# One step of a two-layer recurrent transformer: where turned probabilities and weighted values stand in PSUM, where one addition stands on VectorE, and the order of a few loads and stores

## The chip, the cores and the metric

The kernel runs on one NeuronCore of a Trainium2 chip. TensorE (PE) multiplies matrices, VectorE (DVE) and ScalarE (ACT) copy, add and take exponentials, GpSimd (POOL) does small helper work, and SyncE (SP) issues nearly all DMAs, in the order in which they are written. Results of TensorE land in PSUM, which here is eight banks of 2 KB per partition. The metric is the time of one execution on the device in microseconds (us), and of several executions the median.

## The reference, cut to what matters

The input is a sequence of 2048 rows of width 512. Two layers A (with the same weights) and two layers B (with the same weights) follow each other, each behind a layer norm and with a residual:

```python
x = x + A(layernorm(x)); x = x + B(layernorm(x))
x = x + A(layernorm(x)); x = x + B(layernorm(x))
```

A walks over 64 segments of 32 rows and carries 8 rows of memory from one to the next, so its segments can't run at the same time:

```python
for s in range(64):
    h = concat([mem, xs])                  # 8 + 32 = 40 rows
    q, k, v = h @ Wq, h @ Wk, h @ Wv       # 32 heads of 128
    p = softmax(mask(q @ k.T * scale))     # 40 x 40 for each head
    o = (p @ v) @ Wo                       # 40 rows of 512
    mem, out = o[:8], o[8:]
```

B is a dense layer: `max(x @ w1, 0) @ w2`, with w1 of 512 x 1376.

## The kernel before

**Steps.** The two layers A are interleaved. Step k (`step`, from L920; step 0 is `first_step`, L872) works on segment k of the first A (called layer 0 in the code, a = 0) and on segment k - 3 of the second (a = 1). Between them the dense layer of row block k - 1 is computed in the same step. Steps 3 to 63 have both layers; steps 0 to 2 and 64 to 66 have one and are called `single`.

**A step on PE, in order.** `qk(0)` makes queries and keys of heads 0 to 15 (L570); `scores` (L604) and a softmax follow on DVE, ACT and POOL while PE does `qk(1)`, heads 16 to 31. The first half's probabilities are turned by a DMA (`turn_p`, L677, into `PT0`). PE goes on with `dense_h` (the first dense product, L513), the second half's scores, a late share of the output product (`output_late`, tile `wox`, L390), value products, and `dense_y` (the second dense product, L529). Then `turn_second` turns the second half's probabilities on PE by multiplying them with an identity (tile `tp`, L658) and copies them to `PT_sb` (L664). `weighted_v` multiplies probabilities and values (tiles `pv`, L696): 32 heads for each layer in three groups `PVS` of 12, 12 and 8 heads, heads 0 to 15 from `PT0`, 16 to 31 from `PT_sb`. `outputs` copies them out (L713): for each group the memory rows into `OTm`, then the token rows into `OTx`; with two layers DVE copies layer 0 and ACT layer 1. `output_mem` (tile `wo`, L612) needs all heads of `OTm` in order, and from its result `new_memory` makes the memory rows of the next step; until they are there, PE works on `output_own` (L390). Memory values (`memory_values`, L771) end the step and go through DRAM to reach the value buffer `Vs` in the layout that is wanted (L776, then L781).

**What sets the order.** PE, DVE, SP and POOL run in the order in which the code is written (`tc.manual_schedule`, L1071). ACT's order is planned by the framework. The framework adds a wait wherever an instruction touches a tile that another engine still writes or reads.

**PSUM.** Three banks rotate under the tag "c" (`ps_c`), two under "fill" (`ps_fill`), one holds `wox`, `wo` and some value products (`ps_wo`), and two hold the scores (`sp_banks`); the second of these also takes the dense result, and the first the weighted values of group 0, layer 1. A tile of a rotating pool waits until the tile that had its bank is read out. In a two-layer step `turn_second` uses four tiles of four slots, two of each pool; `weighted_v` puts group 0 (layer 0) and group 1 in "c" and group 2 in "fill". The four copies of turned tiles are ACT, ACT, ACT, DVE.

**Late additions.** `add_late` (L417) adds `wox` to the residual on DVE in two parts of 64 partitions (L423). In steps 4 to 65 both parts stand ahead of `turn_second`.

**The first steps on SP.** Before the dense weights are needed, their buffers `w1_sb` and `w2_sb` hold values on their way to DRAM: `values0` copies a product to such a slot and stores it (L344). Step 0 ends with five of these stores. Step 1 then issues the loads of its values (`load_values`, L741), two stores of memory values (L776), two dense weight loads (`load_w1(0, 1)`, L159), and the two loads of the memory rows (`load_memory_values`, L781), on which its `weighted_v` waits. Four loads of w2 (L162) end step 1. In step 2, which has one layer, `dense_h(1)` comes after a value group (L337).

Of the kernel before, what the change touches and what calls it, by code (L numbers as in the profile page):

```python
# [8 lines left out]
F32 = mybir.dt.float32  # L9
# [13 lines left out]
def kernel(  # L23
# [14 lines left out]
    nc = tc.nc  # L38
# [6 lines left out]
    L = M + SEG  # L45
# [4 lines left out]
    NC4 = Dm // 128  # L50
# [275 lines left out]

    def values0(p, n, lo=0, hi=NC4, pool=None, stage=None, late=False):
        r = 64 * (p % 2)
        if (n, lo) == (0, 0):
            vd0[p] = dram.tile([4, 2, 64, 512], BF, tag="vd0", bufs=6, name="vd0")  # L330
        if lo == 0:
            pool, tag = (pool, "wo") if pool else (ps_fill, "fill")
            vp_tiles[p, n] = pool.tile([128, 512], F32, tag=tag, name="vp")
        vp = vp_tiles[p, n]
        for c4 in range(lo, hi):
            for j in range(2):
                nc.tensor.matmul(vp[64 * j:64 * j + 64, :], lhsT=xT0[p // 2][:, c4, r:r + 64],  # L337
                                 rhs=Wv_sb[:, c4, (n + j) * 512:(n + j + 1) * 512],
                                 start=(c4 == 0), stop=(c4 == NC4 - 1), tile_position=(0, 64 * j))
        if hi < NC4:  # L340
            return
        vst = wk.tile([128, 512], BF, tag="vst", bufs=5, name="vst")[:] if stage is None else stage
        evict(vst, vp[:], late)
        nc.sync.dma_start(out=vd0[p][n // 2].rearrange("j t e -> (j t) e"), in_=vst)  # L344

# [298 lines left out]

    def turn_second(single=False):

        tps = {}
        for u in range(2):
            for g in range(2):
                if single and u:  # L650
                    tps[u, g] = tps[0, g][:, 4:8]
                    continue
                pool, tag = (ps_fill, "fill") if u else (ps_c, "c")
                tps[u, g] = pool.tile([128, 8 if single else 4, L], F32, tag=tag, name="tp")
            for sl in range(4):
                for g in range(2):
                    R = 64 * g
                    nc.tensor.matmul(tps[u, g][:, sl, :], lhsT=P1_sb[R:R + L, 4 * u + sl, :],  # L658
                                     rhs=ident[R:R + L, R:R + L], start=True, stop=True)
        ns = 8 if single else 4  # L660
        for s0 in range(0, 8, ns):
            for g in range(2):
                copy = nc.vector.tensor_copy if g and s0 == 8 - ns else nc.scalar.copy
                copy(out=PT_sb[:, s0:s0 + ns, g, :], in_=tps[s0 // 4, g][:, 0:ns])  # L664

# [206 lines left out]
    def first_step():  # L872
# [5 lines left out]
        with tc.high_priority(offset=PRIO):  # L878
# [19 lines left out]
            memory_values(0, (None, next(slots)), (1,))  # L898
            turn_second(True)
            tokens_in(1)  # L900
# [19 lines left out]
    def step(k):  # L920
# [9 lines left out]
        with tc.high_priority(offset=PRIO):  # L930
# [66 lines left out]
        with tc.high_priority(offset=PRIO):  # L997
# [71 lines left out]

    mom = {}  # L1070
    with tc.manual_schedule(engines={mybir.EngineType.PE, mybir.EngineType.DVE, mybir.EngineType.SP,  # L1071
# [82 lines left out]
```

## Time and profile before

| | |
|---|---|
| median of 3 runs | 1596.98 us (1592.14 to 1597.73) |
| profiled execution | 1600.23 us, of which the span of its instructions is 1598.5 |
| busy, share of the span | PE 98%, DVE 78%, ACT 47%, POOL 19% |
| mean granted TensorE clock | 0.999 of full speed |
| DMA | 144.17 MB, mean 90 GB/s |
| from one step's first turn (`tp`) to the next step's | 23.42 us where nothing disturbs it (937.72 to 961.13) |

A row of a timeline gives the start in us, the length in us, engine, line, operation, tiles as out<-in, shape, how many instructions were merged, and in brackets the idle time before it and what ended that. The rows of PE are modelled: a matmul's row reaches from the start of its input to the end of its output, some 0.18 us for 40 columns, while the next one may start 13 ns later. So the rate is read from starts. A row of stretches gives the stretch, its length, the busy time of PE, PEld, DVE, ACT and POOL with instruction counts, the granted clock, the DMA share and GB/s.

### The profile page before, as it was taken

The numbers are of one execution on the slowest core, as the hardware profiler recorded it, in microseconds if no ns is written. First come the engines' busy times: TensorE is split into PE (matmuls) and PEld (weight loads), VectorE is DVE, ScalarE is ACT, GpSimd is POOL, SyncE is SP. The second block draws the span as 40 slices with busy tenths as digits, with TensorE's granted clock in tenths as the row PEclk, the third lists the DMA queues.
The fourth block names the chain that finished last, engine by engine and source line by source line (L and its number), as shares of the span: only waits on it lengthen the run. The fifth ranks groups of instructions, "written<-read, shape, count | busy, mean of one in ns | idle before, by whom it ended". The sixth has DMA issues, their size and how long they took to land.

```text
span 1598.5 us, 104157 instructions
## 1 busy us (share of the span) xinstructions
PE 1562.6 (98%) x47089; PEld 1302.2 (81%) x47090; DVE 1245.6 (78%) x3526; ACT 745.8 (47%) x1878; POOL 299.8 (19%) x606
## 2 busy tenths in 40 slices
PE   6999999999999999999999999999999999999998
PEld 4678888878888888888887888888888888888876
DVE  4467888878887888887888888788878878878865
ACT  3444454444444445444544544444444454444442
POOL 2011122121112112212111211221211121121110
PEclk9999999999999999999999999999999999999999
DMA  9734234334333433433433434343233324324321
GB/s 370 225 80 82 77 77 89 87 70 87 80 80 82 84 85 71 90 82 73 92 79 78 81 88 81 72 94 80 75 85 76 81 74 85 80 71 86 73 68 39
DMA packets 233547, 144.17 MB, mean 90 GB/s; under 512 B 125032, under 2 KB 229520, under 8 KB 233104
## 3 DMA queue, kind: packets, MB, share of 16 engines
q1 hardware_dynamic: 233008, 137.48, 36.3%
q8 instruction: 369, 6.05, 1.7%
q14 instruction: 74, 0.61, 0.1%
q10 hardware_dynamic: 96, 0.03, 0.0%
HBM read 65.41 MB, written 45.09 MB: 69 GB/s over the span
## 4 chain that ended last, share of the span: by engine, by line
PE 87%; DVE 1%; DMA 1%; issue 1%; POOL 0%; ACT 0%; POOLq 0%; ACTq 0%
PE qp L570 35%; PE wo L612 7%; PE vm L771 7%; PE own L390 7%; PE v L376 6%; PE hp L513 5%; PE sp L529 4%; PE pv L696 4%; PE wox L390 4%; PE sp L604 3%; PE vp L811 3%; PE tp L658 1%; DMA xnT<-XN 1%; PE sp L696 0%; PE mt L835 0%
## 5 line engine op out<-in xcount | busy, mean ns | idle before, releaser
L576 ACT CAST QT<-qp 128x480 bf16<-128x480 f32 (+3 forms) x402 | 200.6, 499 | 394.1 <-PE qp L570 392.3
L570 PE MATMUL qp<-HT,Wq_sb 128*128 128x80 bf16 (+1 forms) x8576 | 368.2, 200 | 2.2 <-POOL HT L757 1.2
L570 PEld LDWEIGHTS <-Wq_sb 128*128 128x128 bf16 x8576 | 323.5, 100 | 33.8 <-issue 28.1
L570 PE MATMUL qp<-HT,Wk_sb 128*128 128x80 bf16 (+1 forms) x8576 | 344.3, 200 | 0.3 <-issue 0.3
L570 PEld LDWEIGHTS <-Wk_sb 128*128 128x128 bf16 x8576 | 317.1, 100 | 0.9 <-issue 0.8
L642 POOL TENSOR_TENSOR P_sb<-es,sm 128x320 bf16<-128x320 f32 x186 | 132.0, 724 | 698.2 <-ACT es L628 399.0
L578 DVE CAST KT<-qp 128x480 bf16<-128x480 f32 (+3 forms) x402 | 220.2, 574 | 28.4 <-PE qp L570 25.0
L622 DVE TENSOR_REDUCE mx<-sp 128x8 f32<-128x320 f32 x256 | 114.4, 487 | 131.1 <-PE sp L604 131.1
L390 PEld LDWEIGHTS <-OTx 128*32 128x32 bf16 x6272 | 157.7, 96 | 27.8 <-issue 10.9
L628 ACT ACTIVATE es<-es 128x320 f32<-128x320 f32 x256 | 109.4, 469 | 69.2 <-DVE es L626 69.1
L390 PE MATMUL own<-Wo_sb,OTx 128*32 128x256 bf16 x4096 | 133.0, 273 | 0.8 <-issue 0.6
L612 PE MATMUL wo<-Wo_sb,OTm 128*32 128x512 bf16 x2112 | 129.2, 383 | 1.4 <-issue 1.2
L771 PE MATMUL vm<-Wv_sb,HTm 128*32 128x512 bf16 x2144 | 129.1, 379 | 0.4 <-issue 0.3
L775 ACT CAST VmS<-vm 128x512 bf16<-128x512 f32 x132 | 77.4, 586 | 104.7 <-PE vm L771 100.8
L638 DVE TENSOR_REDUCE sm<-es 128x8 f32<-128x320 f32 x256 | 117.4, 458 | 10.8 <-ACT es L628 1.8
L376 PE MATMUL v<-Wv_sb,xnT 128*32 128x512 bf16 x2048 | 122.1, 379 | 0.1
L596 DVE CAST sp<-maskb 128x320 f32<-128x320 bf16 x256 | 118.5, 485 | 0.0
L626 DVE TENSOR_TENSOR es<-sp,mx 128x320 f32<-128x320 f32 x256 | 113.2, 482 | 0.5
L288 POOL TENSOR_TENSOR mv<-mv,mhalf_t 128x2 f32<-128x2 f32 (+1 forms) x67 | 45.7, 682 | 306.7 <-DVE mv L287 154.5
L513 PE MATMUL hp<-xnT,w_sb 128*128 128x64 bf16 (+1 forms) x2948 | 96.5, 192 | 0.8 <-DVE xnT L467 0.4
L529 PE MATMUL sp<-w_sb,hT 128*32 128x256 bf16 (+1 forms) x2772 | 92.9, 275 | 1.0 <-ACT hT L519 0.7
L771 PEld LDWEIGHTS <-HTm 128*32 128x32 bf16 x2144 | 59.8, 97 | 41.3 <-issue 2.3
(127 smaller groups left out, 2102.5 us busy)
## 6 DMA issues: line engine op xcount, KB each, us to landing
Vs<-vd SPq DMA_DIRECT2D x96, 256.0 KB
vd<-vst SPq DMA_DIRECT2D x133, 128.0 KB
vmd<-VmS SPq DMA_DIRECT2D x132, 128.0 KB
Vs<-vmd SPq DMA_DIRECT2D x254, 32.0 KB
Vs<-vmd SPq DMA_DIRECT2D x60, 128.0 KB
vd<-vst SPq DMA_DIRECT2D x96, 64.0 KB
Wq_sb<-in_A_Wq_dram SPq DMA_DIRECT2D x2, 2048.0 KB
Wk_sb<-in_A_Wk_dram SPq DMA_DIRECT2D x2, 2048.0 KB
```

The source lines that it names most:

```text
L376: nc.tensor.matmul(vp[32 * j:32 * j + 32, :], lhsT=tokens[c4], rhs=Wv_sb[:, c4, n * 512:(n + 1) * 512], start=(c4 == 0), stop=(c4 == NC4 - ...
L390: nc.tensor.matmul(t[q:q + 32, 0:HALF], lhsT=OTx[:, h, SEG * a:SEG * a + SEG], rhs=Wo_sb[:, h, HALF * j:HALF * j + HALF], start=(h < h0 + ...
L513: nc.tensor.matmul(hp[:, fc - f0, 0:n].rearrange("p (s t) -> p s t", s=ns), lhsT=w1_sb[:, c4, u:u + 128], rhs=cols(c4), start=(c4 == 0), s ...
L529: nc.tensor.matmul(sp_banks[1][32 * q:32 * q + 32, 0:w], lhsT=hT_tiles[d][0:fs, fc, SEG * o:SEG * o + SEG], rhs=w2_flat[0:fs, fc * Dm + HA ...
L570: nc.tensor.matmul(qp[:, hi, 0:ncol], lhsT=W_sb[:, c4, h * Dh:(h + 1) * Dh], rhs=HT[:, c4, a_lo:a_hi, :], start=(c4 == 0), stop=(c4 == NC4 ...
L576: nc.scalar.copy(out=dst[:, 0:nh, a_lo * L:a_hi * L], in_=qp[:, 0:nh, 0:ncol])
L578: nc.vector.tensor_copy(out=dst[:, 0:nh, a_lo * L:a_hi * L], in_=qp[:, 0:nh, 0:ncol])
L596: nc.vector.tensor_copy(out=sp_tiles[a], in_=maskb2)
L612: nc.tensor.matmul(wo[32 * j:32 * j + 32, :], lhsT=OTm[:, h, n, 2 * M * c:2 * M * c + 4 * M], rhs=Wo_sb[:, h, :], start=(h < 4), stop=(h > ...
L638: nc.vector.tensor_reduce(out=sm[:], in_=es[:], axis=AX.X, op=ALU.add)
L642: eng.tensor_tensor(out=P[:, :, 64 * a:64 * a + L], in0=es[:], in1=sm[:].unsqueeze(2).to_broadcast([128, 8, L]), op=ALU.mult)
L771: nc.tensor.matmul(vp[32 * j:32 * j + 32, :], lhsT=HTm[:, c4, :], rhs=Wv_sb[:, c4, n * 512:(n + 1) * 512], start=(c4 == 0), stop=(c4 == NC ...
```

## The change

- `turn_second`: two tiles of eight slots in "c" in every step. In two-layer steps the copies are, in order: ACT (tile 0, slots 0 to 3), DVE (tile 1, slots 0 to 3), ACT (tile 0, slots 4 to 7), ACT (tile 1, slots 4 to 7). What is given as `behind` is called after them.
- `weighted_v`: group 1 (heads 12 to 23) goes to "fill", group 2 to "c".
- `add_late`: the first part stays ahead of `turn_second`; the second stands behind its copies, in steps 4 to 65.
- `values0`: the five last stores of step 0 are kept back and issued in step 1, behind the memory-value stores; `load_memory_values` comes ahead of `load_w1(0, 1)`.
- The last two of four w2 loads move from the end of step 1 to step 2, behind `qk(0)`.
- In step 2 `dense_h` comes ahead of the second half of the value group.

The number and kinds of instructions stay the same on every engine.

```diff
-    def values0(p, n, lo=0, hi=NC4, pool=None, stage=None, late=False):
+    def values0(p, n, lo=0, hi=NC4, pool=None, stage=None, late=False, held=None):
...
-        nc.sync.dma_start(out=vd0[p][n // 2].rearrange("j t e -> (j t) e"), in_=vst)
+        def keep():
+            nc.sync.dma_start(out=vd0[p][n // 2].rearrange("j t e -> (j t) e"), in_=vst)
+        if held is None:
+            keep()
+        else:
+            held.append(keep)
...
-    def turn_second(single=False):
-        tps = {}
-        for u in range(2):
+    def turn_second(behind=None):
+        tps = [ps_c.tile([128, 8, L], F32, tag="c", name="tp") for g in range(2)]
+        for sl in range(8):
             for g in range(2):
-                if single and u:
-                    tps[u, g] = tps[0, g][:, 4:8]
-                    continue
-                pool, tag = (ps_fill, "fill") if u else (ps_c, "c")
-                tps[u, g] = pool.tile([128, 8 if single else 4, L], F32, tag=tag, name="tp")
...
-        ns = 8 if single else 4
-        for s0 in range(0, 8, ns):
-            for g in range(2):
-                copy = nc.vector.tensor_copy if g and s0 == 8 - ns else nc.scalar.copy
-                copy(out=PT_sb[:, s0:s0 + ns, g, :], in_=tps[s0 // 4, g][:, 0:ns])
+        if behind is None:
+            parts = ((0, 0, 8, nc.scalar.copy), (1, 0, 8, nc.vector.tensor_copy))
+        else:
+            parts = ((0, 0, 4, nc.scalar.copy), (1, 0, 4, nc.vector.tensor_copy),
+                     (0, 4, 8, nc.scalar.copy), (1, 4, 8, nc.scalar.copy))
+        for g, lo, hi, copy in parts:
+            copy(out=PT_sb[:, lo:hi, g, :], in_=tps[g][:, lo:hi])
+        if behind:
+            behind()
...
-                    pool, tag = (ps_fill, "fill") if t == 2 else (ps_c, "c")
+                    pool, tag = (ps_fill, "fill") if t == 1 else (ps_c, "c")
...
-                    values0(p, n, stage=next(slots))
+                    values0(p, n, stage=next(slots), held=held)
...
             qks = qk(0, act, behind=behind)
+            if k == 2:
+                load_w2(6, 8)
+                load_w2(8, 10)
...
             if k == 1:
+                for keep in held:
+                    keep()
+                load_memory_values(k, act)
                 load_w1(0, 1)
-                load_memory_values(k, act)
...
+        if k == 2:
+            dense_h(d)
         value_group(k, 0, 2, NC4, late=True)
...
-            if k > 1:
-                dense_h(d)
...
             dense_y(d, 0, NFC)
-            add_late(k)
-        else:
-            add_late(k, (0,))
+        add_late(k, (0,))
...
-            turn_second(single)
+            turn_second(None if single else lambda: add_late(k, (1,)))
+        if single and 1 < k < LAST:
+            add_late(k, (1,))
         if k == 1:
-            for lo, hi in ((0, 3), (3, 6), (6, 8), (8, 10)):
-                load_w2(lo, hi)
+            load_w2(0, 3)
+            load_w2(3, 6)
```

More of the change, by code (lines that the diff above doesn't have):

```diff
@@ L643, in softmax @@
                               in1=sm[:].unsqueeze(2).to_broadcast([128, 8, L]), op=ALU.mult)
-    def turn_second(single=False):
-        tps = {}
-        for u in range(2):
+    def turn_second(behind=None):
+        tps = [ps_c.tile([128, 8, L], F32, tag="c", name="tp") for g in range(2)]
+        for sl in range(8):
             for g in range(2):
-                if single and u:
-                    tps[u, g] = tps[0, g][:, 4:8]
-                    continue
-                pool, tag = (ps_fill, "fill") if u else (ps_c, "c")
-                tps[u, g] = pool.tile([128, 8 if single else 4, L], F32, tag=tag, name="tp")
-            for sl in range(4):
-                for g in range(2):
-                    R = 64 * g
-                    nc.tensor.matmul(tps[u, g][:, sl, :], lhsT=P1_sb[R:R + L, 4 * u + sl, :],
-                                     rhs=ident[R:R + L, R:R + L], start=True, stop=True)
-        ns = 8 if single else 4
-        for s0 in range(0, 8, ns):
-            for g in range(2):
-                copy = nc.vector.tensor_copy if g and s0 == 8 - ns else nc.scalar.copy
-                copy(out=PT_sb[:, s0:s0 + ns, g, :], in_=tps[s0 // 4, g][:, 0:ns])
+                R = 64 * g
+                nc.tensor.matmul(tps[g][:, sl, :], lhsT=P1_sb[R:R + L, sl, :],
+                                 rhs=ident[R:R + L, R:R + L], start=True, stop=True)
+        if behind is None:
[7 more added lines that the diff above has]
+            behind()
     def transpose_p():
@@ L898, in first_step @@
             memory_values(0, (None, next(slots)), (1,))
-            turn_second(True)
+            turn_second()
             tokens_in(1)
@@ L1068, in step @@
             prepare(k + 1)
-    mom = {}
+    mom, held = {}, []
     with tc.manual_schedule(engines={mybir.EngineType.PE, mybir.EngineType.DVE, mybir.EngineType.SP,
```

## The prediction

> **What bounds the kernel now.** I read the page first (busy shares, then the chain that ended last), then the timeline of one ordinary two-layer step engine by engine, then the first 90 us with the load queue and the granted clock.
>
> ```profile
> PE 1562.6 (98%) x47089; PEld 1302.2 (81%) x47090; DVE 1245.6 (78%) x3526; ACT 745.8 (47%) x1878; POOL 299.8 (19%) x606
> ...
> PE 87%; DVE 1%; DMA 1%; issue 1%; POOL 0%; ACT 0%; POOLq 0%; ACTq 0%
> ```
>
> PE is never idle for long and the chain runs over it, so whatever holds PE up is paid in full, once per step. PE rows are modelled, though: a matmul that waits can still look busy. So I read starts, not busy shares. One step, around its turned probabilities (tp, 961.13; below "+" counts us from there), first PE, then ACT, then DVE:
>
> ```profile
> 961.13 0.37 PE L658 MATMUL tp<-ident,P_sb 40*128 40x40 bf16 x16
> ...
> 961.78 0.45 PE L696 MATMUL pv<-PT,Vs 40*128 40x40 bf16 x8
> 962.07 0.56 PE L696 MATMUL pv<-PT_sb,Vs 40*128 40x40 bf16 x32
> 962.56 0.61 PE L612 MATMUL wo<-Wo_sb,OTm 128*32 128x512 bf16 x8
> ```
> ```profile
> 961.43 0.68 ACT L664 CAST PT_sb<-tp 128x160 bf16<-128x160 f32 x3 [0.82 <-PE tp L658]
> 961.99 0.27 ACT L713 CAST OTm<-sp 128x96 bf16<-128x96 f32 x1
> ```
> ```profile
> 960.47 0.88 DVE L423 TENSOR_TENSOR R<-R,wox 64x256 f32<-64x256 f32 x2
> 961.59 0.33 DVE L664 CAST PT_sb<-tp 128x160 bf16<-128x160 f32 x1 [0.24 <-PE tp L658]
> 961.87 0.26 DVE L713 CAST OTm<-pv 128x96 bf16<-128x96 f32 x1
> ```
>
> The 24 matmuls of heads 0 to 11 start between +0.22 and +0.53, one every 13 ns. Heads 12 to 15 (the x8) take from +0.65 to +0.92, where 0.10 would do: their two banks are those of the first turned tiles, and ACT frees them at +0.60 and +0.79. The x32 then run without a hole, every 12.4 ns, and wo starts at +1.43. The two additions (0.88) end before DVE is needed; DVE even waits 0.24. The first DVE copy of the weighted values, on which the first wo weights wait, ends at +1.00 (961.87 + 0.26): DVE has 0.43 us to spare before wo. This is the figure that decides.
>
> The start:
>
> ```profile
> 61.67 0.93 SPq L159 DMA_DIRECT2D w_sb<-in_B_w_dram  x2
> 63.04 0.69 SPq L781 DMA_DIRECT2D Vs<-vmd  x2
> ```
> ```profile
> 67.68 0.57 PE L696 MATMUL pv<-PT,Vs 40*128 40x40 bf16 x16 [1.74 <-DMA Vs<-vmd]
> ...
> 89.70 1.41 PE L529 MATMUL sp<-w_sb,hT 128*32 128x320 bf16 x22 [0.73 <-ACT hT L519]
> ```
> ```profile
> 69.40:72.80 3.40, 3.40 (x55) 1.98 (x48) 0.31 (x1) 0.59 (x1) 0.00 (x0) 0.50 0.89 292
> ```
>
> In step 1 PE waits 1.74 us for the memory rows of the values, which queue behind two dense-weight loads; soon after, the granted clock (third value from the end) is 0.50 for 3.4 us.
>
> **The change, part by part. Two-layer steps.**
>
> *Two banks instead of four.* Every turn now writes one of two whole-bank tiles, and in the built program the first ACT copy waits for the last turn of its tile, not for the fourth. Row for that: in step 1 the turned tile is already whole; turns start at 65.57, the ACT copy at 65.97, so +0.40 instead of +0.30. ACT's three copies (0.68 for three) would end at +1.08. But the third now reads the bank that DVE's copy reads, and the program makes it wait for that copy. The row comes first here: DVE's copy cannot start before +0.46 and takes 0.33, so it ends at +0.79; ACT's third starts about +0.82, takes 0.31 and ends at +1.13. [...]
>
> *Heads 12 to 23 in the fill banks.* Heads 12 to 15 wait for nothing (the value copies that hold these banks end before the turns start), so the 0.32 us hole closes. What is late next: head 16 needs ACT's first copy (+0.69) and head 17 DVE's (+0.79, +0.84 at PE: 0.05 is the lag seen where the second ACT copy, over at +0.79, lets its bank's matmul go at +0.84). Heads 17 to 24 run to about +1.0, head 25 waits for ACT's third copy: +1.13 + 0.05 = +1.18. Fourteen matmuls at 12.4 ns, then the usual 0.105 to wo: +1.45. So without the additions wo would come 0.02 us later than now: the hole only moves.
>
> *The second addition behind the copy.* It leaves a place where it cost nothing (dense matmuls hid it) and now stands between DVE's turned copy and DVE's first copy of weighted values. One addition is 0.42 (0.88 for two with the gap), and a gap of 0.03 stands on either side, as between the two in the 0.88, where today's two copies overlap by 0.05. Chain: 0.79 + 0.03 + 0.42 + 0.03 + 0.26 = +1.53, PE lag 0.05, wo at +1.57 to +1.58 instead of +1.43: **+0.147 us**. Queued behind the addition are all six DVE copies of weighted values; the later ones wait for PE anyway (DVE idles 0.34 before the second), so only the first counts, and all PE work after wo moves with it.
>
> I worked this out on all 62 steps that make the two additions, each with its own starts. 57 come out between +0.12 and +0.17. In three, where the additions already end late, the sum is +0.01 to +0.03. The two single-layer steps near the end gain 0.04 each, since DVE's copy no longer stands behind both additions. Sum **+8.4 us**. Ends: +0.02 per step if the addition finds cover (+1.1 in all); +0.18 if ACT's third copy lags more (+10.8). I take the chain, since each link is a row.
>
> *Step 1, load order.* Five held stores (128 KB each, issue 2.35 together) move on SP past one value load and two memory-value stores; the two memory-row loads move ahead of the two dense loads (344 KB each). Memory rows needed 4.6 us from issue (63.04) to use; 0.69 MB at the 337 GB/s of 70 to 72 us is 2.0 of that, leaving 2.6. Their issue cannot come before the two stores (end 60 to 61.6) plus 2.35, so 63 to 64.7; arrival 65.6 to 67.3 against a need at 65.8. The wait left is 0 to 1.5; I take 0.6, a gain of 1.2 (ends 0 and 1.74). The dense loads, 1 to 2 us later, have cover until 78.9.
>
> *The clock.* Half clock for 3.4 us costs 1.7. Waits of 0.85 (86.7) and 0.73 (89.7) leave the clock at 1.00, so with the wait cut to 0.6 I take all 1.7 (ends 0 and 1.7). [...]
>
> *Step 2.* dense_h (44 matmuls, two ACT passes) moves ahead of half a value group (4 matmuls): the 0.73 wait for hT is covered, but its second pass (0.39) now stands in front of the exponential on ACT, and the probabilities follow; I take -0.45 (ends 0 and -0.73). Two dense loads (256 KB each) move from step 1 past two stores and a block load into step 2, ahead of that step's value load: dense_y needs them at 81.7; ends 0 and +1, I take +0.2, nearer to covered since the same queue was idle by 78. Value loads behind them are used at 91: hidden.
>
> Start in all: -1.2 - 1.7 - 0.45 + 0.2 = **-3.15 us**. Bank changes in step 0 and step 3, which has no additions: within 0.1.
>
> **Sum.** 8.4 - 3.15 = +5.2 us. The profiled execution took 1600.23 (span 1598.5 and 1.7 around it), so 1605.4 for its like; it lies 3.25 above the median of the runs, 1596.98, from which I forecast **1602.2**.
>
> **Rivals.**
> - *The closed hole is the gain (faster).* If DVE's first weighted copy ended before +1.37 and the turned halves came early, wo would start right after ACT's first weighted copy, at +1.18: -0.245 on 60 steps, -14.7, with the start 1579. For it: the hole is real, and DVE idles 0.24 before its copy. Against: the addition needs 0.45 and DVE had 0.43 before wo. It decides at +1.37. Chance 0.10.
> - *The start gives nothing:* 0.64 MB of stores stand where 0.69 MB of weights stood, and the wait stays: 1605.4. For it: SP is in order and issues took 2 us at times (54.16, 63.83). Chance 0.22.
> - *The half clock comes anyway*, from the waits before it and not from this one: -1.45 at the start, 1603.9. The 0.44 and 1.74 us of waiting in step 1 are less than the fall lasts, and 0.47 and 0.37 more came at 57.4 and 62.2. [...] Chance 0.13.
> - *The addition finds cover* (wo's weights not held): +0.02 per step, 1595. Chance 0.12.
> - My forecast 0.40; worse than all of these 0.03.
>
> **How the numbers follow.** What a measurement here can tell from no change is about 0.5%, 8 us: below 1589 is faster, above 1605 slower. Runs of one kernel differ by 5.6. My case reaches above 1605 in a quarter, the second rival in half, the third in a third: slower 0.10 + 0.11 + 0.04 + 0.03 = 0.28; faster 0.10; the rest 0.62. The range 1593 to 1609 holds my case, rivals two and three nearly whole and most of the fourth; the faster rival is left out.
>
> **What will show it.** In a two-layer step: ACT's first turned copy +0.40 after tp instead of +0.30; no hole before heads 12 to 15 but holes before heads 17 and 25; DVE in the order addition, copy, addition, weighted copy; wo at +1.57, its weights' idle put down to DVE OTm; step period 0.15 longer. At the start: the 1.74 wait at 0 to 1.5 and no row at clock 0.50 near 70. wo at +1.43 or before would prove me wrong, as would a wait at the dense_y of step 2 of over 1 us.

## The result, and the profile after

The changed kernel takes 1605.82 us (median of 5 runs, 1603.72 to 1609.62) against 1596.98 (5 runs, 1592.14 to 1597.73): a ratio of 1.0063, with a 95% interval of 1.0042 to 1.0083. That is 10.1 us slower (6.7 to 13.3), where I had forecast 5.2 more. The profiled execution took 1605.82 us, with a span of 1604.1; the one before had a span of 1598.5.

The first lines of the page show that PE was given no more work, and that the chain which ended last is no longer PE alone:

```profile
PE 1562.5 (97%) x47089; PEld 1308.0 (82%) x47090; DVE 1241.8 (77%) x3526; ACT 745.5 (46%) x1878; POOL 299.8 (19%) x606
...
PE 84%; ACT 5%; DVE 1%; issue 1%; POOL 0%; SPq 0%; DMA 0%; POOLq 0%; ACTq 0%
```

An ordinary two-layer step of the changed kernel (first turn at 964.83), on PE, ACT and DVE; columns as in the table's note above. "+" counts from that first turn again.

```profile
964.83 0.37 PE L658 MATMUL tp<-ident,P_sb 40*128 40x40 bf16 x16
...
965.38 0.26 PE L700 MATMUL pv<-PT,Vs 40*128 40x40 bf16 x8
965.58 0.75 PE L700 MATMUL pv<-PT_sb,Vs 40*128 40x40 bf16 x32
966.49 1.91 PE L619 MATMUL wo<-Wo_sb,OTm 128*32 128x512 bf16 x32 [0.16 <-ACT OTx L717]
```
```profile
965.24 0.69 ACT L666 CAST PT_sb<-tp 128x160 bf16<-128x160 f32 x3 [0.93 <-PE tp L658]
965.82 0.24 ACT L717 CAST OTm<-sp 128x96 bf16<-128x96 f32 x1
965.95 0.50 ACT L717 CAST OTx<-sp 128x384 bf16<-128x384 f32 x1
```
```profile
965.27 0.33 DVE L666 CAST PT_sb<-tp 128x160 bf16<-128x160 f32 x1 [0.69 <-PE tp L658]
```

The same stretch of DVE, in a window so narrow that its first weighted copy stands alone:

```profile
965.63 0.42 DVE L430 TENSOR_TENSOR R<-R,wox 64x256 f32<-64x256 f32 x1
966.08 0.26 DVE L717 CAST OTm<-pv 128x96 bf16<-128x96 f32 x1
```

Heads 12 to 15 (the x8) now run on without a hole, from +0.55 to +0.63. The x32 behind them spread over 0.75 us where 0.56 was enough before: there are the two new holes, 0.06 us before head 17 and 0.15 before head 25, and a shorter wait of 0.12 before head 16 for ACT's first copy. Their last matmul starts at +1.32 in both kernels. DVE's chain is copy to +0.76, addition to +1.22, weighted copy to +1.51. wo starts at +1.65; before it was +1.43. wo's wait is put down to ACT's OTx, whose row ends at 966.45. That is not the cause: the load of wo's first weights starts 0.01 us behind that end, where the load that waited for ACT alone started 0.05 behind it (1218.34 after 1218.29, in the experiment with the first copies on ACT). wo starts 0.147 us after the end of DVE's weighted copy in 59 of the 61 two-layer steps. The trace has the wait itself, an instruction of its own at PE's weight loads that lasts 51 ns, and the load behind it:

```profile
L619 PEldq EVENT_SEMAPHORE  x2: 51/51/51, 966.4 to 966.5; - x2
```
```profile
966.46 0.15 PEld L619 LDWEIGHTS <-OTm 128*32 128x32 bf16 x8 [0.24 <-ACT OTx L717]
```

The first of the two stands at 966.38 to 966.43, 0.04 to 0.09 behind DVE's copy, and waits for DVE; the load at 966.46 waits for ACT, of which the copy that it needs ended at 966.06.

Where the time went, from the starts of the first tp and the first wo row of every step in both traces: from tp to wo, steps 3 to 62, +12.86 us (0.228 in an ordinary step); from wo to the next tp, the same steps, -5.99; up to the tp of step 3, -0.32; after the tp of step 63, -0.91. Together +5.6, the difference of the spans. The medians of the runs lie 8.8 apart, since the traced execution before was 3.25 above its median and the one after is its median; where those 3.25 us are is not shown.

The first steps, on SP and PE, and three stretches with the granted clock (third value from the end):

```profile
62.59 0.97 SPq L785 DMA_DIRECT2D Vs<-vmd  x2
63.61 1.74 SPq L159 DMA_DIRECT2D w_sb<-in_B_w_dram  x2
```
```profile
65.79 0.37 PE L658 MATMUL tp<-ident,P_sb 40*128 40x40 bf16 x16 [0.44 <-DVE P_sb L649]
66.01 0.55 PE L700 MATMUL pv<-PT,Vs 40*128 40x40 bf16 x16
...
77.73 0.65 PE L520 MATMUL hp<-xnT,w_sb 128*128 128x32 bf16 x20 [1.07 <-issue]
...
80.39 0.40 PE L536 MATMUL sp<-w_sb,hT 128*32 128x256 bf16 x4 [0.47 <-DMA w_sb<-in_B_w_dram]
81.08 0.51 PE L536 MATMUL sp<-w_sb,hT 128*32 128x256 bf16 x6 [0.30 <-DMA w_sb<-in_B_w_dram]
...
91.72 0.53 PE L700 MATMUL pv<-PT_sb,Vs 40*128 40x40 bf16 x15 [0.35 <-DVE PT_sb L666]
```
```profile
69.80:73.20 3.40, 3.40 (x109) 2.22 (x101) 2.21 (x10) 0.94 (x3) 0.00 (x0) 1.00 0.81 285
1591.10:1594.55 3.45, 1.91 (x59) 1.50 (x52) 2.59 (x11) 0.65 (x2) 2.27 (x3) 1.00 0.00 0
1594.56:1597.97 3.41, 3.03 (x31) 1.80 (x28) 1.01 (x3) 0.00 (x0) 0.06 (x1) 0.50 0.02 5
```

The memory rows are issued at 62.59 and PE no longer waits for them; the half clock near 70 is gone. Step 2 has new waits in their place, and at 1594.56 a stretch at half clock stands near the end that the trace before does not have.

### The profile page after: what moved, and what is told of

The parts are those of the page before. It is cut to its first block, busy times and chain, and to the rows that moved or that the text cites. A ratio compares the mean times of both kernels' runs of the same rounds, so it can differ in the third digit from the quotient of the medians.

```text
span 1604.1 us, 104089 instructions
## 1 busy us (share of the span) xinstructions
PE 1562.5 (97%) x47089; PEld 1308.0 (82%) x47090; DVE 1241.8 (77%) x3526; ACT 745.5 (46%) x1878; POOL 299.8 (19%) x606
## 4 chain that ended last, share of the span: by engine, by line
PE 84%; ACT 5%; DVE 1%; issue 1%; POOL 0%; SPq 0%; DMA 0%; POOLq 0%; ACTq 0%
PE qp L577 36%; PE wo L619 7%; PE vm L775 7%; PE own L397 7%; PE v L383 6%; PE hp L520 5%; PE sp L536 4%; PE wox L397 4%; PE sp L611 3%; PE vp L815 3%; ACT PT_sb L666 3%; PE tp L658 1%; ACT OTm L717 1%; ACT OTx L717 1%; PE mt L839 0%
## 5 line engine op out<-in xcount | busy, mean ns | idle before, releaser
L629 DVE TENSOR_REDUCE mx<-sp 128x8 f32<-128x320 f32 x256 | 114.4, 487 | 131.2 <-PE sp L611 131.2
L619 PEld LDWEIGHTS <-OTm 128*32 128x32 bf16 x2112 | 57.1, 96 | 55.0 <-ACT OTx L717 7.1
```

Source lines behind the costliest of these rows:

```text
L619: nc.tensor.matmul(wo[32 * j:32 * j + 32, :], lhsT=OTm[:, h, n, 2 * M * c:2 * M * c + 4 * M], rhs=Wo_sb[:, h, :], start=(h < 4), stop=(h > ...
```

## The experiments

My theory after the result: the second addition in front of DVE's first weighted copy is the loss in every two-layer step, and it is larger than forecast because wo starts 0.15 us behind that copy and not 0.05. The rival: the shared bank of the turned tiles is the loss. For the start: the gain of step 1 is real but lost again in step 2; the rival is that a single trace before had overstated it. Each ratio below is to the kernel before, run beside it on the same chip; the kernel before had medians of 1599.6 to 1601.4 there, so only ratios are compared.

### Both additions ahead again

```diff
 (changed kernel)
             dense_y(d, 0, NFC)
-        add_late(k, (0,))
+            add_late(k)
+        else:
+            add_late(k, (0,))
...
-            turn_second(None if single else lambda: add_late(k, (1,)))
-        if single and 1 < k < LAST:
-            add_late(k, (1,))
+            turn_second(None if single else lambda: None)
```

> The changed kernel with both additions of a step ahead of the turns again; the two banks, the fill banks and the start stay as changed. Theory (the second addition, in front of the first weighted copy on DVE, is the loss): DVE's turned copy is followed at once by its first weighted copy, so the first matmul of wo comes at about +1.42 after the first turn (the second addition and its gap, 0.45 us, are gone, but head 25 then sets the end at +1.45 by my sum). In the dozen or so steps in which DVE has nothing to cover the additions with, wo stays near +1.66. Over the 62 steps about -10.8 us against the changed kernel: some 1595, ratio to the kernel before 0.997 to 1.001. Rival (the two-bank layout itself is the loss, because heads 17 and 25 wait for the shared bank): wo stays at +1.6 or later and the time at 1604 or above.

Measured: 1605.22 us, ratio 1.0022 (1.0011 to 1.0032). In 33 of the 61 two-layer steps wo comes at +1.42, as the theory says, so against the kernel before the two-bank layout costs nothing there. But in the 28 others it comes at +1.49 to +2.07, on average +1.71, later than in the changed kernel, and the sum from tp to wo is only 6.4 us shorter than there. One of the late steps (first turn at 1503.62), on DVE, ACT and PE:

```profile
1503.50 0.87 DVE L430 TENSOR_TENSOR R<-R,wox 64x256 f32<-64x256 f32 x2
1504.41 0.33 DVE L666 CAST PT_sb<-tp 128x160 bf16<-128x160 f32 x1
```
```profile
1504.77 0.29 ACT L666 CAST PT_sb<-tp 128x160 bf16<-128x160 f32 x1 [0.27 <-DVE PT_sb L666]
```
```profile
1504.79 0.68 PE L700 MATMUL pv<-PT_sb,Vs 40*128 40x40 bf16 x30 [0.24 <-DVE PT_sb L666]
```

Where the additions end late (+0.75 here), DVE's copy is late, ACT's third copy waits 0.27 us for it, as the program has it (the two share a bank), and head 17 waits too (0.24). In 8 of the 28 steps the additions are over by +0.22, and two instructions of the layer norm's statistics (L227, L228) behind them hold DVE until +0.60; in three more both come together. In the kernel before, DVE made the last of the four copies and a late one cost little: wo came within 0.03 of +1.43 in 56 of 61 steps. It is DVE's place as the second to copy that costs, and hardly the shared bank: in the experiment on the hole below, DVE copies second from four separate banks, and in the 23 steps that are late in both, wo averages +1.68 there and +1.70 here. In the changed kernel wo comes at +1.65 in nearly every step, of either kind. The miss of my expectation is that I had counted a dozen late steps and there were 28.

### The second addition behind, nothing else

```diff
 (kernel before)
             dense_y(d, 0, NFC)
-            add_late(k)
-        else:
-            add_late(k, (0,))
+        add_late(k, (0,))
...
             turn_second(single)
+            if 1 < k < LAST:
+                add_late(k, (1,))
```

> The kernel before with one thing changed: the second addition of a step stands behind the turned copies. Four banks of turned probabilities, the fill banks and the start stay as before. Theory (the addition is the loss, whatever the banks): DVE's turned copy 0.46 to 0.78, addition 0.81 to 1.23, first weighted copy 1.26 to 1.52; with the lag of 0.15 us from there to wo that the changed kernel shows, wo at about +1.67 instead of +1.43, +0.24 on some 60 steps = +14.6 us: 1611, ratio 1.008 to 1.010. With the lag of 0.05 that I had assumed, wo at +1.57 and the time near 1606. Rival (the banks are the loss, the addition hides): wo within 0.05 of +1.43 and the time within 3 us of the kernel before.

Measured: 1614.15 us, ratio 1.0077 (1.0059 to 1.0094). wo at +1.67 in the median; the sum from tp to wo grows by 13.9 us, where 14.6 was expected. A step with its first turn at 1224.39, DVE, then DVE in a narrow stretch, then PE and ACT:

```profile
1224.85 0.33 DVE L664 CAST PT_sb<-tp 128x160 bf16<-128x160 f32 x1 [0.25 <-PE tp L658]
```
```profile
1225.20 0.42 DVE L423 TENSOR_TENSOR R<-R,wox 64x256 f32<-64x256 f32 x1
1225.66 0.26 DVE L713 CAST OTm<-pv 128x96 bf16<-128x96 f32 x1
```
```profile
1226.06 0.83 PE L612 MATMUL wo<-Wo_sb,OTm 128*32 128x512 bf16 x12 [0.17 <-ACT OTm L713]
```
```profile
1225.25 0.66 ACT L713 CAST OTm<-sp 128x96 bf16<-128x96 f32 x2
```

wo starts 0.14 us after DVE's weighted copy (1225.92), as in the changed kernel (0.15 after 966.34). ACT's second copy here ends at 1225.91, 0.15 before wo, but in the changed kernel 0.04 before it: the lag that stays the same is the one behind DVE. The lag behind DVE is 0.145 to 0.147 in 60 of the 61 two-layer steps. So the added wait, and its lag, need neither the two banks nor the fill banks. The ratio, 12.3 us, is more than the trace shows (13.9 from tp to wo, less 5.0 in the rest of the step); some of it is the clock, whose mean over these runs was 0.9972 against 0.9983 for the kernel before (an estimate of some 1.9 us, since a stretch of 3.41 us at half clock costs 1.7 and takes 0.001 off the mean).

### The start alone

```diff
 (kernel before)
-                    values0(p, n, stage=next(slots))
+                    values0(p, n, stage=next(slots), held=held)
...
+            if k == 2:
+                load_w2(6, 8)
+                load_w2(8, 10)
...
-                load_w1(0, 1)
+                for keep in held:
+                    keep()
                 load_memory_values(k, act)
+                load_w1(0, 1)
...
+        if k == 2:
+            dense_h(d)
         value_group(k, 0, 2, NC4, late=True)
...
-            if k > 1:
-                dense_h(d)
...
-            for lo, hi in ((0, 3), (3, 6), (6, 8), (8, 10)):
-                load_w2(lo, hi)
+            load_w2(0, 3)
+            load_w2(3, 6)
```

> The kernel before with only the start changed: the stores of the memory values ahead of the dense weights in step 1, two loads of dense weights moved to step 2, and in step 2 the first dense layer ahead of half a value group. The two-layer steps are as before. By my prediction's sum the start gives -3.15 us: 1593.8, ratio 0.998. By the trace of the changed kernel (wait for the memory rows gone and the clock at 1.00, but 0.47 and 0.30 us of waits for the dense weights and some 1.7 us of PE holes in step 2 come in their place) it gives -0.3: ratio 1.000. Told apart by the timeline of steps 1 and 2: whether step 2 still has the waits at dense_y when nothing else is changed.

Measured: 1601.69 us, ratio 1.0008 (0.9996 to 1.0021). The forecast 0.998 is excluded. Of step 2's waits in the changed kernel, the ones for the dense weights do not appear (dense_y runs through from 79.29), but one put down to issue does, before the first dense product:

```profile
77.96 0.65 PE L520 MATMUL hp<-xnT,w_sb 128*128 128x32 bf16 x20 [1.21 <-issue]
```

This wait takes back part of what step 1 wins: with the new start it is 0 to 1.21 us, on average 0.92 over the seven traces with it, and with the old start 0 to 0.89, on average 0.39 over five. What holds PE there is not shown.

### The memory rows first, nothing else

```diff
 (kernel before)
-                load_w1(0, 1)
                 load_memory_values(k, act)
+                load_w1(0, 1)
```

> The kernel before with one change at the start: in step 1 the loads of the memory rows are issued ahead of the first dense weights; the stores stay where they are. By my prediction's terms the wait of 1.74 us shrinks and the half clock after it does not come: up to -1.2 - 1.7 = -2.9 us, ratio 0.998. Rival, from the run with the whole start changed (ratio 1.0008): what is won in step 1 is lost again in step 2, where the dense weights then come late: ratio 1.000, with waits of 0.3 to 0.8 us at the dense layers of step 2 in the timeline.

Measured: 1601.75 us, ratio 1.0006 (0.9993 to 1.0019): nothing won here either. The trace, taken from the slowest of the 11 runs (1604.51), has 0.23 us of waiting left for memory rows, but 2.21 us of issue at the first dense product, and three stretches at half clock:

```profile
67.88:71.29 3.41, 3.41 (x49) 1.89 (x45) 0.47 (x2) 0.59 (x1) 0.00 (x0) 0.50 0.83 254
...
81.54:84.94 3.40, 3.40 (x54) 2.32 (x51) 0.98 (x2) 0.52 (x2) 0.00 (x0) 0.50 0.07 20
...
91.78:95.18 3.40, 3.20 (x50) 2.19 (x51) 1.74 (x6) 0.35 (x2) 1.23 (x4) 0.50 0.22 58
```

So a half clock came near 68 with next to nothing left of the wait that I had held responsible. And the wait itself differs where its code does not. Here is step 1 of the second experiment, whose start is that of the kernel before, on PE:

```profile
65.80 0.37 PE L658 MATMUL tp<-ident,P_sb 40*128 40x40 bf16 x16 [0.44 <-DVE P_sb L642]
66.83 0.57 PE L696 MATMUL pv<-PT,Vs 40*128 40x40 bf16 x16 [0.66 <-DMA Vs<-vmd]
```

Over the five executions traced with the old start the wait was 1.74 (the one that I predicted from), 0.66, 0.70, 0.82 and nothing. With the new start it was nothing in seven of seven. The tp of step 3 stood at 115.72, 113.93, 115.52, 114.83 and 113.54 with the old start (mean 114.7), and between 113.08 and 115.40 with the new one (mean 114.4).

### Everything but the start

```diff
 (changed kernel: the edits of "the start alone" undone)
```

> The changed kernel with the start of the kernel before: only the turns, the banks and the additions are changed. It measures the start's share within the whole change (whole change: ratio 1.0063). By my prediction the start gives -3.15 us, so that without it the ratio would be 1.0083; by the run with the start alone (ratio 1.0008, interval 0.9996 to 1.0021) the start gives nothing or costs up to 3, so that the ratio would be 1.0043 to 1.0063. wo in the two-layer steps should stay at +1.65 in either case.

Measured: 1607.74 us, ratio 1.0046 (1.0032 to 1.0059), so 5.1 to 9.4 us over the kernel before; wo at +1.65. The 1.0083 that my start term asked for is excluded. The turns and additions make up the loss; the start did not hide part of it.

### The first weighted copies on ACT

```diff
 (changed kernel)
-            return engines[a if len(act) == 2 else t % 2](out=dst, in_=src)
+            first = len(act) == 2 and t == 0 and hi == M
+            return engines[1 if first else a if len(act) == 2 else t % 2](out=dst, in_=src)
```

> The changed kernel with the first copy of weighted memory values (the one on which wo's first weights wait) on ACT instead of DVE, in both layers. The addition stays behind DVE's turned copy. Theory 1 (the lag of 0.15 us between DVE's copy and wo is there because the first weights of wo wait for two engines, one of them in an instruction of its own): wo's first weights now wait for ACT alone, whose two copies follow its third turned copy (1.09) and the weighted values (1.32 at the latest matmul); wo at about +1.49 with a lag of 0.05, 0.16 earlier than in the changed kernel, -9.5 us: 1596, ratio 1.000. Theory 2 (the lag is a property of any wait there): wo at +1.59 and the time near 1602, ratio 1.003. Rival (the two-bank layout holds the weighted values themselves up, not the addition): wo stays at +1.63 or later.

Measured: 1597.98 us, ratio 0.998 (0.9968 to 0.9992). wo at +1.41 to +1.43 in 56 of 61 steps, earlier than either theory said, because I had put the end of the weighted values and of ACT's copies too late. A step with its first turn at 1216.92: ACT in a narrow stretch, DVE, PE.

```profile
1217.90 0.24 ACT L718 CAST OTm<-pv 128x96 bf16<-128x96 f32 x1
1218.03 0.26 ACT L718 CAST OTm<-sp 128x96 bf16<-128x96 f32 x1
```
```profile
1217.71 0.42 DVE L430 TENSOR_TENSOR R<-R,wox 64x256 f32<-64x256 f32 x1
1218.17 0.50 DVE L718 CAST OTm<-pv 128x96 bf16<-128x96 f32 x2
```
```profile
1217.66 0.75 PE L700 MATMUL pv<-PT_sb,Vs 40*128 40x40 bf16 x32
1218.34 1.05 PE L619 MATMUL wo<-Wo_sb,OTm 128*32 128x512 bf16 x16
```

The addition still ends at +1.22 and DVE's copies still follow it; but nothing that starts wo waits for them. wo starts 0.05 us after ACT's second copy (1218.29) and 0.11 after the last weighted value, the usual distance. In the built program its first weights now wait for one engine, where in the changed kernel they wait for DVE in an instruction of its own and then for ACT; the trace has that instruction before the first wo in all 61 two-layer steps there, and only in one here. That fits a lag of 0.15 for two engines and 0.05 for one; but here PE would have started at +1.425 for its own part too, so the lag is bounded by this run (0.05 or less) and not measured by itself.

### The hole before heads 12 to 15

```diff
 (kernel before; early is set in steps 5 to 60)
-                copy = nc.vector.tensor_copy if g and s0 == 8 - ns else nc.scalar.copy
+                by_dve = g and s0 == (0 if early else 8 - ns)
+                copy = nc.vector.tensor_copy if by_dve else nc.scalar.copy
```

> The kernel before with one change: of the four copies of turned probabilities, DVE makes the second instead of the last, in the steps whose dense work hides the additions. It tests whether the hole of 0.32 us before heads 12 to 15 is worth anything. Theory (PE's own order sets wo once DVE and ACT are early): the second bank is free at +0.72 to +0.78 instead of +0.79, so heads 12 to 15 end some 0.05 to 0.10 earlier and wo comes at +1.33 to +1.37: -3 to -5 us, ratio 0.997 to 0.998. Rival (ACT's last copy, now behind two of its own, holds the last heads): wo stays at +1.42 or later, ratio 1.000.

Measured: 1602.54 us, ratio 1.001 (0.9998 to 1.0021). The new order applies in steps 5 to 60, not only where dense work hides the additions. In 31 of them wo moves from +1.43 to +1.32, more than the theory gave; in the other 25 it averages +1.66, because DVE is still busy when it should copy the second tile, with the additions (16 steps, three of them with the layer norm's statistics behind), with the statistics behind additions that were over in time (8), or with additions that end at +0.36 (one). A step of the second kind, first turn at 1221.88, DVE:

```profile
1221.67 0.87 DVE L423 TENSOR_TENSOR R<-R,wox 64x256 f32<-64x256 f32 x2
1222.57 0.33 DVE L665 CAST PT_sb<-tp 128x160 bf16<-128x160 f32 x1
```

So the hole is worth 0.11 us a step, in the steps where DVE is free. In the same steps the two-bank layout with both additions ahead stood at +1.42, so against this order the two banks give that 0.10 away. Four banks with DVE second in these steps alone was not run.

### Heads by bank

```diff
 (kernel with the first weighted copies on ACT)
-            parts = ((0, 0, 4, nc.scalar.copy), (1, 0, 4, nc.vector.tensor_copy),
-                     (0, 4, 8, nc.scalar.copy), (1, 4, 8, nc.scalar.copy))
+            parts = ((0, 0, 4, nc.scalar.copy), (1, 0, 8, nc.vector.tensor_copy),
+                     (0, 4, 8, nc.scalar.copy))
...
+        if len(act) == 2:
+            tiles.sort(key=lambda th: (PVS[th[0]][0] + th[1] >= 16 and 1 + (PVS[th[0]][0] + th[1]) % 2))
```

> The kernel with the first weighted copies on ACT (wo at +1.425, PE waiting 0.15 us before head 25 for ACT's third turned copy, which waits for DVE's copy of the same bank), changed so that no bank is read by both engines: ACT copies its bank in two halves, DVE its bank in one piece, and the last 16 heads are computed in the order of the banks, the eight of ACT's bank first. Theory (the shared bank is what holds head 25): ACT's second half ends at +0.89, its heads run to +1.04, DVE's whole bank is copied by about +0.93, the other eight heads run to +1.24 and wo starts at about +1.35: -4.5 us against the kernel it is made from, ratio to the kernel before 0.995. Rival (the second addition, now ending at +1.38, comes back as the wait through the later weighted copies, or the eight heads from one bank run slower): wo at +1.42 or later, ratio 0.998.

Measured: 1597.42 us, ratio 0.9982 (0.9972 to 0.9993). The new sort takes heads 16 to 31 by bank, the eight of bank 0 first. The weighted values end 0.06 earlier (last start +1.26, forecast +1.24), but wo stays at +1.44. Its first turn is at 1216.47; DVE, then PE:

```profile
1216.90 0.49 DVE L666 CAST PT_sb<-tp 128x320 bf16<-128x320 f32 x1 [0.24 <-PE tp L658]
1217.43 0.42 DVE L430 TENSOR_TENSOR R<-R,wox 64x256 f32<-64x256 f32 x1
```
```profile
1217.21 0.69 PE L704 MATMUL pv<-PT_sb,Vs 40*128 40x40 bf16 x32
1217.90 1.48 PE L619 MATMUL wo<-Wo_sb,OTm 128*32 128x512 bf16 x23
```

The addition ends at 1217.85 and wo starts 0.05 later: wo writes the bank that the addition reads. So the addition holds wo by a second road, which had no effect while the weighted copy behind it was later still.

### The turns by bank too

```diff
 (the last kernel)
-        for sl in range(8):
-            for g in range(2):
+        for g, sl in (((g, sl) for sl in range(8) for g in range(2)) if behind is None else
+                      ((g, sl) for g in range(2) for sl in range(8))):
```

> As the last one, and the turns are made bank by bank too: all eight of ACT's bank first. ACT can then start its first copy 0.1 us earlier (+0.30 instead of +0.40). Theory: ACT's halves end at +0.59 and +0.79, the heads of its bank run to +0.94, those of DVE's bank from about +0.98 to +1.18, wo at +1.29: -8 us against the kernel with the first copies on ACT, ratio to the kernel before 0.993. Rival: turns that use the same rows of PE one after another run slower than alternating ones (0.012 us each in the traces so far); at twice that the turns end 0.2 us later, and wo comes at +1.45 or later, ratio 0.999 or above.

Measured: 1602.0 us, ratio 1.001 (0.9997 to 1.0022), wo at +1.53: the rival. The last turn starts at +0.31 instead of +0.19, on average 0.021 us for each turn instead of 0.013. In both traces the starts read as two series of eight, each with one start every 0.025 us: alternating turns run both series side by side, bank by bank they overlap only from +0.12 to +0.19. So DVE's bank is copied 0.09 later, and with it the addition ends at +1.47; wo follows it by 0.05. ACT's first copy starts at +0.40 as before, so nothing was won on the other side.

### The second addition ahead where that is early

```diff
 (heads by bank)
-        add_late(k, (0,))
+        ahead = 1 < k < LAST and (single or k not in LATE)
+        add_late(k, (0, 1) if ahead else (0,))
...
-            turn_second(None if single else lambda: add_late(k, (1,)))
+            turn_second(None if single else lambda: None if ahead else add_late(k, (1,)))
...
+    LATE = {4, 5, 8, 9, 12, 13, 15, 17, 19, 21, 22, 25, 26, 29, 33, 36, 37, 40, 41, 43, 45, 47, 50, 54, 57, 61, 62, 63}
```

`LATE` holds the steps in which DVE's work ahead of its copy, the additions or the statistics behind them, ended late in the runs with both ahead.

> The kernel ordered by bank (wo at +1.436, where the trace shows the second addition ending at +1.380 and wo's first matmul 0.056 behind it, since wo writes the bank that the addition reads), with the second addition put ahead of the turns again in those 33 two-layer steps in which the earlier runs show the additions over in time, and in the three single-layer steps; in the 28 others it stays behind the copies. Theory (in this order of heads nothing but the addition holds wo): in the 33 steps the weighted values end at +1.254 as now and wo starts 0.105 later, at +1.36; -0.076 on 33 steps = -2.5 us, ratio to the kernel before 0.9966. Rival 1 (ACT's first weighted copies hold wo instead): wo at +1.25 + 0.05 or earlier is not reached, they end at +1.20, so this is excluded unless they move. Rival 2 (what wo gains comes back as waits of PE's weight loads that the trace puts down to issue, 4 to 7 us in kernels with wo at +1.42 against 1.3 to 1.8 with wo at +1.65): ratio 0.998.

Measured: 1592.58 us (5 runs, 1592.21 to 1597.38), ratio 0.9961 (0.9947 to 0.9975): 6.2 us faster than the kernel before, and the lowest ratio of all, though its interval overlaps those of its neighbours. wo at +1.364 in exactly the 33 steps, +1.45 on average in the others. A step with its first turn at 1236.62, PE and DVE:

```profile
1237.36 0.69 PE L704 MATMUL pv<-PT_sb,Vs 40*128 40x40 bf16 x32
1237.98 1.26 PE L619 MATMUL wo<-Wo_sb,OTm 128*32 128x512 bf16 x20
```
```profile
1235.95 0.88 DVE L430 TENSOR_TENSOR R<-R,wox 64x256 f32<-64x256 f32 x2
1237.05 0.49 DVE L666 CAST PT_sb<-tp 128x320 bf16<-128x320 f32 x1 [0.23 <-PE tp L658]
```

The same kernel with the start of the kernel before:

> The fastest kernel so far (heads by bank, second addition ahead of the turns where that is early; ratio 0.9961 to the kernel before, interval 0.9947 to 0.9975) with the start of the kernel before. A second measurement of the start's share. If the changed start costs 1 to 3 us, as the runs with the start alone (1.0008) and with everything but the start (1.0046 against 1.0063) have it, the ratio falls to 0.9945 to 0.9955. If the start gives the 3.15 us of my prediction, it rises to 0.998. If it does nothing: 0.996. wo at +1.37 in the two-layer steps in any case.

Measured: 1595.28 us, ratio 0.9975 (0.9962 to 0.9988). The point values would give the changed start a gain of 2.2 us; the two intervals overlap. Alone it came out at a loss of 1.3, and within the whole change (1.0063 against 1.0046) at a loss of 2.7. The traces do not put the 2.2 us at the start either: the tp of step 3 stands at 113.54 here and at 114.31 with the changed start. So the start is worth nothing that these runs can tell, somewhere between a gain of some 2 us and a loss of some 3.

## Why the prediction was right, and where it was not

The forecast 1602.2 was in the right direction and the time inside the range, but most of its terms were wrong and leaned against each other. In the traces the difference is +5.6 us and the forecast +5.2, and that closeness is luck: the chain in steps 3 to 63 cost 4.6 us more than forecast, the start gave 2.8 us less, the rest of the two-layer steps, on which I had put nothing, gave 6.0, and what follows step 63 another 1.1.

- **Two banks.** ACT's first copy starts at +0.40 (forecast +0.40), its third ends at +1.09 (forecast +1.13), the holes moved from heads 12 to 15 to heads 17 and 25, and the weighted values end where they did. Right. That the third copy waits for DVE's is the program's own doing; no run lets two engines read one bank at once, so what the chip would do then is not shown.
- **The second addition.** The chain to the end of DVE's weighted copy came out at +1.51 (forecast +1.53). The term that was mis-sized is the PE lag: 0.15 us and not 0.05, in the changed kernel and in the second experiment alike. I had taken 0.05 from a matmul that waits for one engine; the first weights of wo wait for two, for DVE in an instruction of its own. By the same lag DVE had some 0.28 us to spare before wo and not the 0.43 of my figure "that decides". So an ordinary step lost 0.228 and not 0.147, and the steps 3 to 63 together 13.05 and not 8.4.
- **The rest of the step**, which I had left unchanged, became 6.0 us shorter, so that the step's period grew by 0.11 and not by 0.15. The profile has PE's weight loads of the two output products, before and after:

```profile
L390 PEld LDWEIGHTS <-OTx 128*32 128x32 bf16 x6272 | 157.7, 96 | 27.8 <-issue 10.9
L612 PEld LDWEIGHTS <-OTm 128*32 128x32 bf16 x2112 | 51.5, 96 | 48.8 <-issue 5.5 <-DVE OTx L713 0.3
```
```profile
L397 PEld LDWEIGHTS <-OTx 128*32 128x32 bf16 x6272 | 159.2, 96 | 23.6 <-issue 9.0 <-DVE R L548 0.5
...
L619 PEld LDWEIGHTS <-OTm 128*32 128x32 bf16 x2112 | 57.1, 96 | 55.0 <-ACT OTx L717 7.1 <-ACT OTm L717 7.1 <-issue 2.3
```

  Idle time put down to issue falls from 16.4 to 11.3 us. Part of it comes as a few irregular stops of 0.2 to 1.5 us ahead of weight loads inside wo and own. Where wo starts at +1.65 or +1.67 (the changed kernel, everything but the start, the second addition behind) the stops of over 0.2 us cost 1.3, 2.3 and 2.4 us over steps 4 to 61, and the rest of the step sums to 1315 to 1317 us over steps 3 to 62; in the ten others, with wo at +1.32 to +1.53 in the median, they cost 3.6 to 6.1, and the sum is 1318 to 1324. So on average some 5 us of what the later wo loses comes back in the rest of the step, some 3 of them in these stops. What makes these stops shorter where wo comes later is not shown.
- **Step 1, load order**, -1.2: right that the wait goes, wrong in its size, because 1.74 was the longest of five. Their mean is 0.8.
- **The clock**, -1.7: the step that failed. I took the half clock for the sure result of that wait. With the old start it stood at 67 to 70 us in the three executions with waits of 0.70, 0.82 and 1.74, and not in the two with 0.66 and none; with the rows first it stood there behind a wait of 0.23. With the new start it is gone from that place in all seven, but came later in two (79.11 and 86.61). Before 100 us the old start had four such stretches in five executions and the new one two in seven. By these counts the term is some 0.9 us (an estimate from few traces), and in one execution it is 1.7 or nothing.
- **Step 2**, -0.45 and +0.2: the wait of 0.73 for hT went in all seven, but the probabilities come later as I had said, and in six of the seven tp (0.23) and the weighted values (0.25 to 0.35, since DVE's turned copy stands behind other work) wait instead. The wait put down to issue before the first dense product, 0.5 us longer on average with the new start, was in no term. Dense weights came late once (0.77 us together, the changed kernel), inside my ends.
- **Sum of the start**, -3.15: measured between -2.2 and +2.7 by three pairs of kernels. Taking it as nothing, my own terms would have given 1605.4, the second rival.
- **The closed hole as the gain**: did not happen in the changed kernel, for the reason given (wo needs the copy behind the addition). The experiments show that the gain is there: with the additions out of the way of wo it was worth 0.06 to 0.11 us a step.

## What to carry to other kernels

Ahead of a move on an engine that is off the critical path, list everything that PE's next instruction waits for there, in tiles and in banks. Here one 0.42 us addition held wo by the copy behind it and, when that was cured, by the bank that it reads. Whether a place is free differs from step to step: DVE was free in time behind both additions in 33 steps and late in 28, and choosing by step gave 0.9961 where the same kernel with the second addition behind in every step gave 0.9982 (the intervals touch; both ahead in every step was not run in that layout). A wait that is read from one traced execution is one draw: the 1.74 us that carried my start term was 0 to 0.8 in the four others.

## What the runs showed of the hardware that I had not expected

- **The half clock came in stretches of 3.41 us, and three in one execution stood whole multiples of that apart.** With the rows first they start at 67.88, 81.53 and 91.77 (13.65 and 10.24 apart, 4 and 3 times 3.41). In the last step PE does nothing for 1.54 us in both kernels (to 1593.97 in the changed kernel, to 1589.62 in the kernel before); the clock fell to 0.50 at 1594.56 in the changed kernel and stayed at 1.00 up to 1595.10 in the kernel before. How busy PE was in the 3.4 us ahead does not decide it alone: the clock fell behind 1.91 of 3.45 us (the changed kernel, to 1594.55), 1.71 of 3.41 (the kernel before, to 69.39) and 2.65, 1.19 and 2.19 of 3.40 (the rows first, to 67.87, 81.52 and 91.76), and stayed behind 2.05 of 3.40 (the kernel before, to 1591.70). What decides it is not shown.
- **Runs with a lower mean clock were longer.** In 35 runs of the kernel before on one chip, those with a mean granted clock of 1.000 averaged 1598.8 us, 0.999 1600.2, 0.998 1602.5, and 0.997 or less 1604.3; one stretch of 3.41 us at 0.50 takes 0.001 off the mean clock (1.7 of some 1600 us).
- **wo came 0.1 us later behind DVE where that wait stood in an instruction of its own.** Where the first weights of wo wait for two engines, the wait for DVE stands ahead of the weight load (51 ns in the changed kernel), and wo started 0.147 and 0.146 us behind DVE's copy (the changed kernel, the second addition behind). Where the weights wait for ACT alone and the matmul itself waits for DVE's addition, wo started 0.053 and 0.054 behind it (heads by bank, turns by bank).
- **Turns of one half of PE's rows started every 0.025 us, and alternating halves ran side by side**: 0.013 us for each turn then, and 0.021 in the experiment that made them half after half. There the turns of one half also write one bank, so that rows and bank are not told apart.
